# Gated SSM mix: small unfolding transfers become one VectorE transpose a unit, and two sets of coefficient transfers change queue

## The chip, the cores and the metric

The kernel runs on one core of a Trainium2 chip. The metric is device time in microseconds (us) of one execution. Three runs of the kernel before took 557.36, 558.36 and 561.56 us, median 558.36 us. The profile comes from another execution, which took 563.64 us; the traced span of it is 561.9 us.

## The reference, cut to what matters

All activations are [1, 2048, 1024] in bf16. Two sequence mixers are computed from `x` and mixed by a gate of one number per row:

```python
x = A_x
g = _sigmoid((x * gate_w).sum(-1, keepdims=True))
a = _A_ref(x, ...)   # diagonal complex state space: Bu = x B_bar; h_t = Lam_bar h_{t-1} + Bu_t
                     # y = 2 Re(h C) + x * Dskip
b = _B_ref(x, ...)   # k_shift = 4-tap causal filter of k; kv = k_shift * v
                     # y = (kv convolved with ssm_k, by FFT of length 2S) + kv * ssm_D; q * y with q = x
return g * a + (1 - g) * b
```

The change lies in the second mixer, in the long convolution of `kv` with `ssm_k`, channel by channel over 2048 time steps.

## The kernel before, in words

The kernel works on two streams of instructions at once. The **S5 stream** (branch a) does the input product, L974, L977 and L983 (with L1027 and L1030 the four-step recurrence), over 8 blocks of 128 states, spills half of the states to DRAM (`h_scr`), and later does the output product, L1180, in 16 output tiles. The **convolution stream** (branch b) treats the 1024 channels in 8 units of 128. For one unit it loads k and v transposed (L594), filters and multiplies them on VectorE and ScalarE (L767 to L782), re-sorts them by one VectorE transpose (L747), loads the unit's `ssm_k` (L596, tensor `in_B_ssm_k_dram`), and goes through two matmul stages, L792 and L814, into the spectrum. A unit's spectrum is handled in four quarters, q = 0 to 3. For a quarter a transfer pair *turns* the spectrum (two 128 KB transfers between the halves of the partitions, `turn`), VectorE multiplies the two spectra (L832), and TensorE goes back with 16 matmuls (L842, `inverse`).

Behind the inverse stands the step that changes. The result of one quarter lies in PSUM as 128 partitions by 8 by 128 values. ScalarE or VectorE copies it to a tile `qq` (L601, `evac`). Then each of the 8 slices of `qq`, 128 partitions by 128 values, is *unfolded*: one transfer of 32 KB writes it into 4 partitions of the tile `zb`, with 8 KB in each. That is 8 transfers a quarter, 32 a unit and 256 in all. When all 32 of a unit have landed, the last matmul stage of the unit can start, L871 in `final`, after the bias products L865. VectorE then multiplies by x (L877), and the result is stored to `pB_scr` or, for late units, added to the other branch (L885).

The order of the work is set by a planner that runs when the kernel is built (`_Plan.schedule`). Each operation has an engine, a planned duration, tiles that it reads and writes, and a priority from the tables at the top (`PR`); some may go to a second engine. The planner gives tiles their places in 11 slabs of SBUF of 16 KB a partition (named slab with a number in the instruction lists; one slab holds several tiles), with a cap on how many tiles of a kind live at once (`CAPS`). What comes out is a fixed order for each engine and queue. Each engine and each queue works strictly in that order. Transfers are issued from two queues, SyncE (SP) and GpSimd (POOL); in the instruction lists a queue's transfers take eight semaphores in turn (DMAHW0 to 7 on SP, DMASW0 to 7 on POOL), and a transfer waits for the one that used its semaphore before.

At the start, small vectors of coefficients are worked out on VectorE and ScalarE (L493 to L569, tiles `dco`, `cco`, `gl`). Four transfers of them (`sco<-gl`, L571) bring them to the places where L935 uses them to build diagonal matrices; four more (`sdm`, L455) load `ssm_D`. Both sets stand in the program outside the planner's list, `sco` on SP and `sdm` on ScalarE's queue.

Of the kernel before, what the change touches and what calls it, by code (L numbers as in the profile page):

```python
# [10 lines left out]
ACT = mybir.ActivationFunctionType  # L11
BF16 = mybir.dt.bfloat16
F32 = mybir.dt.float32
# [17 lines left out]
    ],  # L31
# [9 lines left out]
    ],  # L41
    "PO": [
        [-401.7, -1412.4, -159.9],
        [50.8, -104.2, 167.5],
        [-577.2, 239.1, 83.1],
        [-145.7, 329.3, -432.6],
        [-347.1, -38.2, -1031.0],
        [5.0, -1786.7, -451.4],
        [-167.3, -1738.4, -1777.2],
        [-61.5, -1003.4, -1714.9],  # L50
        [157.5, -1495.4, 707.1],
        [176.9, -2338.1, -833.4],
        [45.7, -155.1, 1169.1],
        [189.6, -2590.2, -800.3],
        [-1397.7, -1777.0, -1501.8],
        [-141.1, 180.0, 145.9],
        [-1242.8, -2235.0, -1579.5],
        [-371.1, 54.1, 18.8],
    ],
    "PC": [  # L60
        [163.7, 1215.5],
        [4.1, 1203.7],
        [292.7, 1155.8],
        [-809.1, 841.3],
        [-2711.0, 848.5],
        [-1268.2, 974.9],
        [-1197.3, 881.5],
        [-1623.9, 942.0],
    ],
# [321 lines left out]
def kernel(  # L391
# [20 lines left out]
    nc = tc.nc  # L412
# [41 lines left out]
    for i in range(4):  # L454
        nc.scalar.dma_start(out=sdm[32 * i:32 * i + 1], in_=B_ssm_D.rearrange("(o u q c) -> q o u c", o=1, q=4, c=32)[i])  # L455
# [112 lines left out]
    for k in range(2):  # L568
        cp(gco[:, :, k], cco[:, :, k:k + 2])  # L569
        for h in range(2):  # L570
            nc.sync.dma_start(out=sco[64 * k:64 * k + 64, :, h], in_=vab[64 * h:64 * h + 64, k])  # L571
# [28 lines left out]
    def evac(o_, i_, r, w, prio):  # L600
# [13 lines left out]
    CAPS = {"cA": 3, "qi": 3, "zb": 3, "Hc": 10, "tab": 26, "z": 2, "kv": 27, "qq": 13, "ra": 1, "rb": 11, "kT": 1, "vT":  # L614
            19, "acc": 7, "ka": 1, "va": 1, "pp": 1, "tmpj": 2, "t1": 2, "ot": 5, "BT": 2, "xs": 16, "dg": 3, "dp": 20,
            "tgZ": 32, "frt": 2, "rqt": 13, "Hk": 34, "CT": 9, "ga": 1}
    SPARE, NBIG, NKEEP = 9, 0, 4
# [122 lines left out]
    def conv():  # L740
# [10 lines left out]
        def load_K(u, pr, prt):  # L751
            t = pl.tile("cA", [2 * NJ, 64], cap=CAPS["cA"])
            ex = [(xT[0], 1)] if u < 2 else []
            src = B_ssm_k[u * CH:(u + 1) * CH, :].rearrange("(q c) (n m) -> q n c m", q=4, m=64)
            dma("POOL", 5.0, lambda: [t.ap[32 * q:32 * q + 32] for q in range(4)], lambda: [src[q] for q in range(4)], ex, [t], pr, n=4, alt="SP")
            op("POOL", 0.3, lambda: G.tensor_tensor(out=t.ap[:, :, 0], in0=t.ap[:, :, 0], in1=sdm[:, u, :], op=ALU.add),
               r=[t], w=[t], prio=prt)
            return t
# [76 lines left out]
        def inverse(kv, zb, q, pr):  # L835
            ps = pl.psum([8, CH])
            qq = pl.tile("qq", [8, CH], cap=CAPS["qq"])

            def f():
                for i in range(8):  # L840
# [3 lines left out]
            evac(lambda: qq.ap.rearrange("p k (c j g) -> p k c j g", c=4, g=2),  # L844
                 lambda: ps.ap.rearrange("p k (g j c) -> p k c j g", g=2, c=4), r=[ps], w=[qq], prio=pr)
            for h in range(2):
                dma("SP", 0.65, lambda h=h: [zb.ap[8 * q + 4 * h + i:128:32].rearrange("s r n c -> s (r n) c") for i in range(4)],
                    lambda h=h: [qq.ap[:, 4 * h + i] for i in range(4)], [qq], [(zb, (q, h))], pr, n=4, issue=0.6, alt="POOL", alt_issue=0.65)
# [44 lines left out]
        for u in range(NU):  # L893
# [3 lines left out]
            va = vas[u]  # L897
            zb = pl.tile("zb", [2, 16, CH], cap=CAPS["zb"])
# [4 lines left out]
            for hh in range(2):  # L903
                z = zz[hh]
                for q in (2 * hh, 2 * hh + 1):
# [6 lines left out]
                    inverse(kv, zb, q, pr + 3.0)  # L912
# [3 lines left out]
    def s5():  # L916
# [10 lines left out]
        def diag(pi, pr):  # L927
            res = []
            for tg, (a, b) in (("dp", (0, 3)), ("dg", (3, 5))):
# [13 lines left out]
                op("DVE", 0.95, mk(V), r=[e_dco], w=[dg], prio=pr, alt=("POOL", 1.9, mk(G), PUNTIL))  # L943
# [267 lines left out]
    for end in ends:  # L1211
        end()
    pl.least = {"dsk": 3, "tg1": 0, "tg2": 8, "tg3": 2, "tg4": 2, "tg5": 2, "BT": 7, "dp": 0, "dg": 5, "tab": 4, "Hc": 0,
                "grow": 4, "gb": 2, "gt": 0, "ra": 0, "rb": 0, "Hk": 0, "kT": 4, "tmpj": 0, "cA": 0, "zb": 0, "z": 0, "xs": 0,
                "Hr": 3, "CT": 2, "ot": 7, "ga": 0}
# [5 lines left out]
    order = pl.schedule({"DVE": 9.8, "ACT": 9.5, "PE": 4.6, "POOL": 3.0, "SP": 0.7})  # L1221
# [34 lines left out]
```

## Time and profile before

| | |
|---|---|
| median of 3 runs | 558.36 us (557.36 to 561.56) |
| the profiled execution, its span | 563.64 us, 561.9 us |
| TensorE (PE) matmuls | 395.5 us, 70% of the span |
| VectorE (DVE) | 287.6 us, 51% |
| ScalarE (ACT) | 251.6 us, 45% |
| GpSimd (POOL) | 189.6 us, 34% |
| the 16 DMA engines | 56.4% for SP's queue, 25.0% for POOL's |
| mean granted TensorE clock | 0.86 |

No engine is busy for the whole span, so the shares alone do not say what sets the time. The work of the two streams is spread unevenly, each engine waits in its own order, and the time is read from the gaps: which wait of TensorE is long, who releases it, and what that one waited for.

### The profile page before, as it was taken

What the parts mean: (1) busy time and instruction counts of PE and PEld (TensorE: products, weight loads), DVE (VectorE), ACT (ScalarE), POOL (GpSimd) and SP (SyncE); (2) the same over time, 40 slices, a digit from 0 to 9 for tenths busy, and PEclk for the clock granted to TensorE, in tenths of its full rate; (3) what the DMA queues carried; (4) which work ended last, traced back from release to release, by engine and by line L of the source; (5) the groups of instructions that cost most, each with busy time, mean ns of one, the idle gap of its engine ahead of it and who ended that gap; (6) DMA issues with size and microseconds to landing.
All of it is one profiled execution on the core that took longest, in us unless ns stands there. A gap on an engine that the chain in (4) does not pass through costs nothing. (4 is left out here: it accounts for less than half of the span.)

```text
span 561.9 us, 12598 instructions
## 1 busy us (share of the span) xinstructions
PE 395.5 (70%) x5195; PEld 274.3 (49%) x5216; DVE 287.6 (51%) x392; ACT 251.6 (45%) x325; POOL 189.6 (34%) x271
## 2 busy tenths in 40 slices
PE   4817989999897069497073399399937769865927
PEld 3302443444554045244062298288825658754816
DVE  2159989989993075186223280753104337613413
ACT  2009968978975036079063043275701245702000
POOL 3047500120456027014164064145611622733300
PEclk9966999999999569799576599789987888977969
DMA  6953984755879748789848999799989695997956
GB/s 123 167 93 60 147 132 86 217 151 113 152 109 111 130 122 112 82 174 223 222 57 119 145 152 104 125 187 119 124 121 128 95 145 134 107 146 88 112 112 152
DMA packets 160033, 73.01 MB, mean 130 GB/s; under 512 B 138532, under 2 KB 150852, under 8 KB 159464
## 3 DMA queue, kind: packets, MB, share of 16 engines
q1 hardware_dynamic: 147768, 49.29, 56.4%
q0 software_dynamic: 12080, 22.91, 25.0%
q8 instruction: 41, 0.67, 0.6%
q14 instruction: 16, 0.13, 0.1%
q10 hardware_dynamic: 128, 0.01, 0.0%
HBM read 19.44 MB, written 14.70 MB: 61 GB/s over the span
## 5 line engine op out<-in xcount | busy, mean ns | idle before, releaser
L601 ACT CAST slab<-ps 128x1024 bf16<-128x1024 f32 x136 | 132.1, 1031 | 176.3 <-PE ps L842 117.1
L596 POOL DMA_DIRECT2D slab<-slab x152 | 101.5, 674 | 177.8 <-ACT slab L601 106.2
L1180 PE MATMUL ps<-slab,slab 128*128 128x256 bf16 x960 | 121.5, 284 | 1.6 <-ACT slab L803 1.5
L1180 PEld LDWEIGHTS <-slab 128*128 128x128 bf16 x1024 | 103.2, 102 | 24.4 <-issue 7.6
L974 PE MATMUL ps<-slab,slab 128*128 128x512 bf16 x368 | 89.4, 391 | 25.5 <-ACT slab L601 16.1
L842 PE MATMUL ps<-slab,tG 128*128 128x128 bf16 x512 | 41.4, 252 | 61.9 <-DVE slab L832 57.7
L974 PEld LDWEIGHTS <-slab 128*128 128x128 bf16 x384 | 37.3, 100 | 73.5 <-issue 30.5
L842 PEld LDWEIGHTS <-tG 128*128 128x128 bf16 x512 | 38.4, 115 | 65.6 <-DVE slab L832 37.0
L832 DVE TENSOR_TENSOR slab<-slab 128x2048 bf16<-128x2048 bf16 x32 | 38.2, 1221 | 55.3 <-DMA slab<-slab 53.8
L803 ACT CAST slab<-ps 128x512 bf16<-128x512 f32 x96 | 49.6, 626 | 15.0 <-PE ps L792 15.0
L1189 DVE SCALAR_TENSOR_TENSOR slab<-ps,gcols,slab 128x256 bf16<-128x256 f32 x32 | 15.4, 482 | 58.0 <-PE ps L1180 36.2
L877 DVE TENSOR_TENSOR slab<-ps,slab 128x1024 bf16<-128x1024 f32 x16 | 18.9, 1220 | 41.4 <-PE ps L871 21.7
L814 PE MATMUL ps<-slab,tF 64*128 64x128 bf16 x1024 | 35.9, 228 | 4.0 <-ACT slab L803 2.0
L871 PE MATMUL ps<-slab,tabG 32*32 32x128 bf16 x1024 | 12.3, 274 | 37.3 <-DMA slab<-slab 19.4
L814 PEld LDWEIGHTS <-tF 64*128 64x128 bf16 x1024 | 32.3, 101 | 8.7 <-issue 7.2
L601 DVE CAST slab<-ps 128x1024 bf16<-128x1024 f32 x24 | 28.8, 1218 | 14.6 <-ACT slab L601 9.0
L977 PE MATMUL ps<-slab,slab 128*64 128x512 bf16 x256 | 30.4, 381 | 1.4 <-DMA slab<-in_A_B_re_dram 0.8
L803 DVE CAST slab<-ps 128x512 bf16<-128x512 f32 x32 | 20.3, 685 | 21.2 <-PE ps L792 21.2
L935 DVE TENSOR_TENSOR slab<-id,sco 128x512 bf16<-128x512 bf16 (+1 forms) x11 | 8.8, 801 | 42.2 <-DMA slab<-slab 23.8
L1185 ACT ACTIVATE slab<-ps,gcols 128x256 bf16<-128x256 f32 x31 | 14.7, 475 | 34.9 <-PE ps L1180 34.8
L871 PEld LDWEIGHTS <-tabG 32*32 32x32 bf16 x1024 | 10.4, 95 | 39.5 <-issue 23.3
L596 POOL DMA_DIRECT2D slab<-in_B_ssm_k_dram x28 | 22.1, 796 | 18.7 <-DVE slab L782 7.2
(183 smaller groups left out, 445.7 us busy)
## 6 DMA issues: line engine op xcount, KB each, us to landing
slab<-slab SPq DMA_DIRECT2D x36, 128.0 KB
slab<-slab SPq DMA_DIRECT2D x132, 32.0 KB
slab<-h_scr SPq DMA_DIRECT2D x8, 512.0 KB
slab<-slab POOLq DMA_DIRECT2D x124, 32.0 KB, 7.3
slab<-in_B_ssm_k_dram POOLq DMA_DIRECT2D x28, 128.0 KB, 6.6
slab<-slab POOLq DMA_DIRECT2D x28, 128.0 KB, 8.0
slab<-in_A_x_dram POOLq DMA_DIRECT2D x24, 128.0 KB, 8.8
h_scr<-slab POOLq DMA_DIRECT2D x3, 1024.0 KB, 5.2
```

Of the source, the lines that this page charges most:

```text
L596: QS[q].dma_start(out=o_, in_=i_)
L601: op("ACT", 1.04, lambda: A.copy(o_(), i_()), r=r, w=w, prio=prio, alt=("DVE", 1.2, lambda: V.tensor_copy(o_(), i_())))
L803: return lambda: [fn(put(hh), get(hh)) for hh in range(2)]
L814: PE_.matmul(ps.ap[:, g, i, :], lhsT=tF[64 * g:64 * g + 64, k1, 64 - 64 * r:192 - 64 * r], rhs=z.ap[64 * g:64 * g + 64, k1 % 16, r].rearra ...
L832: TT(out=t, in0=t, in1=kv.ap[:, 1].rearrange("p i c -> p (i c)").unsqueeze(1).to_broadcast([128, 2, 8 * CH]), op=ALU.mult)
L842: PE_.matmul(ps.ap[:, i], lhsT=tG[:, 8 * q + i, b, :], rhs=kv.ap[:, 2 * b, i, :], start=(b == 0), stop=(b == 1))
L871: PE_.matmul(ps[q // 2].ap[32 * e:32 * e + 32, q % 2, n], lhsT=tabG[32 * q:32 * q + 32, b, 4 * n + e, :], rhs=zb.ap[32 * q:32 * q + 32, b, ...
L877: op("DVE", 1.23, lambda h=h, hs=hs: TT(out=xs.ap[:, hs], in0=ps[h].ap.rearrange("p a g c -> p (a g) c"), in1=xs.ap[:, hs], op=ALU.mult), ...
L974: PE_.matmul(ps.ap[:, k], lhsT=BT.ap[:, d, k].rearrange("p r c -> p (r c)"), rhs=t.ap[:, d], start=(d == 0), stop=(d == ND - 1))
L977: PE_.matmul(ps.ap[64 * h:64 * h + 64, k], lhsT=BT.ap[:, d, h, k, :], rhs=t.ap[:, d], start=(d == 0), stop=False)
L1180: PE_.matmul(ps.ap, lhsT=Hr[pi].ap[:, ri, j, a * 128:(a + 1) * 128], rhs=t.ap[:, k_, ri], start=(i == 0 and ri == 0), stop=(i == NP - 1 an ...
L1189: op("DVE", 0.46, lambda: STT(out=ot.ap[:, a, :], in0=ps.ap, scalar=col(gcols, 4 * j + a), in1=ot.ap[:, a, :], op0=ALU.mult, op1=ALU.add), ...
```

## The change: what it does

The copy out of PSUM now writes a tile of the whole unit, `qq` of 64 by 32 by 2 values a partition, one quarter after the other, so that pairs of bf16 values stand side by side. When the four quarters are there, one VectorE transpose of the unit (new function `unfold`, in 32 by 32 blocks of 4-byte pairs, 2048 of them a partition) writes `zb`. The 256 unfolding transfers are gone. The transfers of `sco` and `sdm` are now operations of the planner on POOL's queue, and the operations that use them wait for them in the plan. All priorities (`PR`), the caps and the reserves of the planner have other numbers, and so the order of all the work is another; the table rows are left out here.

```diff
-    for i in range(4):
-        nc.scalar.dma_start(out=sdm[32 * i:32 * i + 1], in_=B_ssm_D.rearrange("(o u q c) -> q o u c", o=1, q=4, c=32)[i])
...
-        for h in range(2):
-            nc.sync.dma_start(out=sco[64 * k:64 * k + 64, :, h], in_=vab[64 * h:64 * h + 64, k])
...
+    kh = [(k, h) for k in range(2) for h in range(2)]
+    e_sco, e_sdm = pl.ext("sco"), pl.ext("sdm")
+    dma("POOL", 0.2, lambda: [sco[64 * k:64 * k + 64, :, h] for k, h in kh], lambda: [vab[64 * h:64 * h + 64, k] for k, h in kh], [e_dco], [e_sco],
+        -1999, n=4, alt="SP")
+    dma("POOL", 0.1, lambda: [sdm[32 * i:32 * i + 1] for i in range(4)],
+        lambda: [B_ssm_D.rearrange("(o u q c) -> q o u c", o=1, q=4, c=32)[i] for i in range(4)], [], [e_sdm], -250, n=4)
...
-        def inverse(kv, zb, q, pr):
+        def inverse(kv, qq, q, pr):
             ps = pl.psum([8, CH])
-            qq = pl.tile("qq", [8, CH], cap=CAPS["qq"])
...
-            evac(lambda: qq.ap.rearrange("p k (c j g) -> p k c j g", c=4, g=2),
-                 lambda: ps.ap.rearrange("p k (g j c) -> p k c j g", g=2, c=4), r=[ps], w=[qq], prio=pr)
-            for h in range(2):
-                dma("SP", 0.65, lambda h=h: [zb.ap[8 * q + 4 * h + i:128:32].rearrange("s r n c -> s (r n) c") for i in range(4)],
-                    lambda h=h: [qq.ap[:, 4 * h + i] for i in range(4)], [qq], [(zb, (q, h))], pr, n=4, issue=0.6, alt="POOL", alt_issue=0.65)
+            evac(lambda: qq.ap[:, :, 8 * q:8 * q + 8, :].rearrange("p (c j) k g -> p c j k g", c=4),
+                 lambda: ps.ap.rearrange("p k (g j c) -> p c j k g", g=2, c=4), r=[ps], w=[(qq, q)], prio=pr)
+
+        def unfold(qq, zb, pr):
+            def f():
+                i = qq.ap.rearrange("p c k g -> p c (k g)").bitcast(F32)
+                o = zb.ap.rearrange("p r n c -> p (r n) c").bitcast(F32).rearrange("p x c -> p c x")
+                V.transpose(o, i)
+            op("DVE", 3.75, f, r=[qq], w=[zb], prio=pr)
...
+            qq = pl.tile("qi", [64, 32, 2], cap=CAPS["qi"])
             zb = pl.tile("zb", [2, 16, CH], cap=CAPS["zb"])
...
-                    inverse(kv, zb, q, pr + 3.0)
+                    inverse(kv, qq, q, pr + 3.0)
+            unfold(qq, zb, PU[u][16])
             final(zb, u, PU[u][10:12], PU[u][12:14])
...
-                op("DVE", 0.95, mk(V), r=[e_dco], w=[dg], prio=pr, alt=("POOL", 1.9, mk(G), PUNTIL))
+                op("DVE", 0.95, mk(V), r=[e_dco, e_sco], w=[dg], prio=pr, alt=("POOL", 1.9, mk(G), PUNTIL))
```

Two places of the new order. The first is the start of the SP queue. Before, the four transfers of `sco` stand behind all loads of x but one:

```order
L594 DMA_TRANSPOSE slab_228<-in_A_x_dram 128x8x256 x2
L594 DMA_TRANSPOSE slab_229<-in_A_x_dram 128x8x256 x2
L594 DMA_TRANSPOSE slab_231<-in_A_x_dram 128x8x256
L571 DMA sco<-gl 64x8x10 x4
L594 DMA_TRANSPOSE slab_231<-in_A_x_dram 128x8x256
L594 DMA_TRANSPOSE slab_231<-in_B_k_dram 128x2048
```

Now they stand on POOL's queue (iota fills index tables, `skb` and the Dskip row are other small loads, L961 builds a table):

```order
L691 IOTA slab_218 128x32
L592 DMA skb<-in_B_shift_k_dram 128x8x4
L592 DMA sdm<-in_B_ssm_D_dram 1x8x32 x4
L592 DMA slab_218<-in_A_Dskip_dram 128x1024
L592 DMA sco<-gl 64x8x10 x4
L961 TENSOR_SCALAR slab_218<-iota_row,phn 128x512
```

SP now goes from the loads of x straight to those of k and v. The second place is the first unit's end, on VectorE. Before, a product that builds a diagonal matrix (L935) goes into a slab that holds the unit's `zb`, and waits for sixteen transfers; behind it stand the products of the spectra, L832:

```order
L601 CAST slab_234<-ps_105 128x2x4x2x64 [waits PE_49]
L1009 SCALAR_TENSOR_TENSOR slab_230<-r_160,slab_236 128x512 [waits DVE_49] x2
L935 TENSOR_TENSOR slab_232<-id_100,sco 128x768 [waits DMAHW0_49,DMAHW1_49,DMASW7_49,DMAHW2_49,DMASW6_49,DMAHW3_49,DMASW5_49,DMAHW4_49,DMASW4_49,DMAHW5_49,DMASW3_49,DMAHW6_49,DMASW2_49,DMAHW7_49,DMASW1_49,DMASW0_49]
L832 TENSOR_TENSOR slab_233<-slab_233 128x2x1024 [waits DMAHW7_49,DMAHW6_49,Activation_49]
L935 TENSOR_TENSOR slab_227<-id_100,sco 128x512
```

Now the first unit's end on VectorE reads as follows (L834 is the product of the spectra, L852 the new transpose, L882 the multiplication by x that follows the last matmuls):

```order
L834 TENSOR_TENSOR slab_224<-slab_224 128x2x1024 [waits DMASW7_49,DMASW0_49,Activation_49]
L961 TENSOR_SCALAR slab_224<-iota_row,phn 128x512
L962 TENSOR_SCALAR slab_218<-slab_224 128x512 [waits DVE_49]
L963 TENSOR_TENSOR slab_224<-slab_224,slab_218 128x512 [waits DVE_49]
L597 CAST slab_219<-ps_101 128x2x512 [waits PE_49,Activation_49]
L852 STREAM_TRANSPOSE slab_225<-slab_224 128x64x32 [waits DMASW6_49,Activation_49]
L882 TENSOR_TENSOR slab_223<-ps_104,slab_223 128x1024 [waits PE_49]
L882 TENSOR_TENSOR slab_223<-ps_101,slab_223 128x1024 [waits PE_49]
```

The transpose waits for the copies of ScalarE and one transfer, and the instruction after it on VectorE waits for TensorE alone. In the lists as a whole the transfers on SP go from 358 to 219 and those on POOL from 240 to 127; there are 64 turning transfers in both, 36 on SP and 28 on POOL before, 32 and 32 now.

## Rows read from the trace of the kernel before

**Rows 1.** The page: span; busy time, share and instructions of each engine.

```profile
span 561.9 us, 12598 instructions
PE 395.5 (70%) x5195; PEld 274.3 (49%) x5216; DVE 287.6 (51%) x392; ACT 251.6 (45%) x325; POOL 189.6 (34%) x271
```

**Rows 2.** Three windows: length; busy time per engine; granted clock, DMA share, GB/s.

```profile
46.00:180.00 134.00, 125.72 (x1077) 61.54 (x1087) 121.10 (x144) 113.72 (x126) 44.59 (x56) 0.98 0.74 132
180.00:562.00 382.00, 250.12 (x3968) 201.63 (x3976) 149.46 (x170) 130.12 (x182) 130.73 (x197) 0.82 0.87 131
532.00:541.00 9.00, 2.74 (x39) 2.14 (x36) 0.97 (x2) 0.00 (x0) 0.00 (x0) 0.88 0.33 54
```

**Rows 3.** The waits: waiting engine and line <- releaser: us, times, longest.

```profile
PE ps L842 <- DVE slab L832: 57.7, 6, 22.3
DVE slab L832 <- DMA slab<-slab: 53.8, 8, 16.3
```

**Rows 4.** Line L596 on SP: issues (ns min/median/max), then who waited (us, times).

```profile
L596 SPq DMA_DIRECT2D slab<-slab x168: 461/594/7627, 139.3 to 540.7; - x168
  PE ps L871: 36.8, 4
  DVE slab L935: 23.8, 1
```

**Rows 5.** DMA issues: transfers, KB each, median us to landing where known.

```profile
slab<-slab SPq DMA_DIRECT2D x132, 32.0 KB
slab<-slab POOLq DMA_DIRECT2D x124, 32.0 KB, 7.3
```

**Rows 6.** Timeline of the start: start us, length, engine, line [idle before <- releaser].

```profile
15.27 0.25 DVE L569 COPY gco<-cco 128x16 f32<-128x16 f32 x2
...
16.61 12.73 SPq L594 DMA_TRANSPOSE slab<-in_A_x_dram  x5
...
29.46 2.78 SPq L571 DMA_DIRECT2D sco<-gl  x4
32.28 2.08 SPq L594 DMA_TRANSPOSE slab<-in_A_x_dram  x1
33.91 0.96 DVE L935 TENSOR_TENSOR slab<-id,sco 128x768 bf16<-128x768 bf16 x1 [18.39 <-DMA sco<-gl]
...
38.88 0.23 ACT L671 ACTIVATE slab<-slab 128x32 f32<-128x32 f32 x1 [26.02 <-DVE slab L661]
```

**Rows 7.** Timeline of TensorE: five long gaps.

```profile
45.95 7.71 PE L974 MATMUL ps<-slab,slab 128*128 128x512 bf16 x24 [15.80 <-ACT slab L601]
...
202.18 3.60 PE L842 MATMUL ps<-slab,tG 128*128 128x128 bf16 x32 [22.33 <-DVE slab L832]
...
281.64 5.94 PE L842 MATMUL ps<-slab,tG 128*128 128x128 bf16 x64 [15.56 <-DVE slab L832]
...
362.62 0.61 PE L865 MATMUL ps<-slab,gl 1*128 1x128 bf16 x16 [9.04 <-DVE slab L803]
...
425.31 1.89 PE L842 MATMUL ps<-slab,tG 128*128 128x128 bf16 x16 [13.07 <-DVE slab L832]
```

**Rows 8.** Timeline of the SP queue: three stretches of issues.

```profile
291.81 21.52 SPq L596 DMA_DIRECT2D slab<-slab  x12
...
412.57 11.17 SPq L596 DMA_DIRECT2D slab<-slab  x12
...
525.98 15.29 SPq L596 DMA_DIRECT2D slab<-slab  x16
```

**Rows 9.** Groups by line and shape: busy us, mean ns of one, idle before.

```profile
L747 DVE STREAM_TRANSPOSE slab<-slab 128x1024 f32<-128x1024 f32 x8 | 16.7, 2087 | 1.2 <-PE ps L842 1.2
L596 POOL DMA_DIRECT2D slab<-slab x152 | 101.5, 674 | 177.8 <-ACT slab L601 106.2 <-DVE slab L1017 23.1 <-DMA slab<-slab 15.6
L474 ACT ACT_TABLE_LOAD x1 | 1.3, 1283 | 8.3 <-DMA sdm<-in_B_ssm_D_dram 8.3
```

**Rows 10.** Line L596 on POOL: one group of issues, ns min/median/max.

```profile
L596 POOL DMA_DIRECT2D slab<-slab x152: 518/686/1196, 142.0 to 526.3; - x152
```

More of the change, by code (lines that the diff above doesn't have):

```diff
@@ L22 @@
     "PS": [
[8 rows of a table removed]
[8 rows of a table added]
     ],
     "PU": [
[8 rows of a table removed]
[8 rows of a table added]
     ],
     "PO": [
[L43 to L58, printed above, removed]
+        [-210.2, -73.8, -86.1],
+        [-291.9, 162.6, -816.3],
+        [5.3, 3.0, 86.8],
+        [40.4, -792.0, 293.9],
+        [5.4, -665.2, -2370.0],
+        [-196.3, -138.6, -221.6],
+        [-193.1, -1372.7, 15.9],
+        [-1456.9, 411.3, -1527.6],
+        [-987.0, 96.5, -1431.0],
+        [128.3, 145.3, 120.7],
+        [235.0, 359.4, -1623.9],
+        [254.4, -728.7, -202.8],
+        [-1445.7, -121.0, -1445.7],
+        [-27.1, 250.0, 381.7],
+        [364.4, -32.7, -138.4],
+        [-1432.1, 112.6, 67.5],
     ],
     "PC": [
[L61 to L68, printed above, removed]
-    ],
-    "PH": [185.9, 238.0, 107.1, 241.4, -7.0, 244.8, 148.7, 248.2],
-    "PG": [-1217.7, -1744.7, -425.8, -200.7, 114.8, -176.6, -514.0, -1241.0],
-    "PX": [39.737, 1.001],
+        [215.4, 379.5],
+        [-242.5, 225.6],
+        [273.9, 453.1],
+        [-604.2, 20.1],
+        [23.6, 121.0],
+        [-129.4, -26.3],
+        [-876.0, 432.9],
+        [364.9, 489.1],
+    ],
+    "PH": [195.4, 194.8, 206.9, 201.9, 0.9, 209.1, -308.5, 216.3],
+    "PG": [-1045.8, -1044.5, -873.4, -710.4, -133.7, 60.4, -820.0, -1425.3],
+    "PX": [44.946, 1.039],
 }
@@ L613 @@
     PS, PU, PO, PC, PH, PG, PX = (PR[k] for k in ("PS", "PU", "PO", "PC", "PH", "PG", "PX"))
[L614 to L617, printed above, removed]
+    CAPS = {"cA": 4, "qi": 5, "zb": 17, "Hc": 4, "tab": 10, "z": 2, "kv": 4, "qq": 9, "ra": 14, "rb": 4, "kT": 2, "vT": 2,
+            "acc": 1, "ka": 1, "va": 1, "pp": 1, "tmpj": 2, "t1": 2, "ot": 3, "BT": 2, "xs": 2, "dg": 20, "dp": 14, "tgZ":
+            12, "frt": 17, "rqt": 14, "Hk": 5, "CT": 9, "ga": 7}
+    SPARE, NBIG, NKEEP = 1, 0, 4
     QB, QA = "POOL", "SP"
@@ L756, in load_K @@
             op("POOL", 0.3, lambda: G.tensor_tensor(out=t.ap[:, :, 0], in0=t.ap[:, :, 0], in1=sdm[:, u, :], op=ALU.add),
-               r=[t], w=[t], prio=prt)
+               r=[t, e_sdm], w=[t], prio=prt)
             return t
@@ L1212 @@
         end()
-    pl.least = {"dsk": 3, "tg1": 0, "tg2": 8, "tg3": 2, "tg4": 2, "tg5": 2, "BT": 7, "dp": 0, "dg": 5, "tab": 4, "Hc": 0,
-                "grow": 4, "gb": 2, "gt": 0, "ra": 0, "rb": 0, "Hk": 0, "kT": 4, "tmpj": 0, "cA": 0, "zb": 0, "z": 0, "xs": 0,
-                "Hr": 3, "CT": 2, "ot": 7, "ga": 0}
+    pl.least = {"dsk": 7, "tg1": 3, "tg2": 5, "tg5": 3, "tgZ": 3, "dp": 2, "dg": 2, "frt": 2, "rqt": 2, "tab": 0, "Hc": 2, "gb":
+                4, "gt": 0, "rb": 0, "Hk": 0, "kT": 0, "qi": 0, "zb": 0, "z": 0, "kv": 0, "xs": 5, "Hr": 0, "CT": 0, "ga": 0}
     RANK = (("ot",), ("CT", "Hr"), ("kT", "vT"), ("acc",), ("tmpj",), ("cA",), ("z",), ("kv",), ("t1",), ("qi","qq",), ("zb",), ("xs", "ga"),
@@ L1220 @@
     pl.spare, pl.nbig, pl.horizon, pl.bias = SPARE, NBIG, PX[0], PX[1]
-    order = pl.schedule({"DVE": 9.8, "ACT": 9.5, "PE": 4.6, "POOL": 3.0, "SP": 0.7})
+    order = pl.schedule({"DVE": 10.7, "ACT": 8.5, "PE": 4.6, "POOL": 3.0, "SP": 0.7})
     with tc.manual_schedule():
```

32 rows, old and new, of the table PR are left out of this document.

## The prediction

> **What bounds the kernel now.** I read the page first. TensorE is the busiest engine and still idle for 561.9 - 395.5 = 166 us; no other engine is near the span [rows 1]. So the time lies in TensorE's gaps, and the second view, the windows, says where: from 46 to 180 us TensorE works 125.7 of 134 us, beside VectorE with 121.1 and ScalarE with 113.7, while from 180 us to the end it works 250 of 382 us, and there the DMA engines are busy 0.87 of the time [rows 2]. The third view is the list of waits. TensorE's inverse (L842) waits 57.7 us, six times, for the product of spectra (L832), and that one waits 53.8 us for transfers from slab to slab, the turning transfers [rows 3]. The fourth is the SP line itself: for transfers issued there the last stage of a unit (L871) waits 36.8 us in four places, and VectorE once for 23.8 us [rows 4]. These are the transfers that the change takes away, 132 on SP and 124 on POOL [rows 5], or others that stand behind them. So the middle of the kernel is bound by computing, its start and its last two thirds by waits for transfers in order.
>
> **The change, part by part.**
>
> *The start.* The coefficients are complete at about 15.5 us, but SP issues their transfers at 29.5, behind loads of x, and VectorE gets them at 33.9; ScalarE's first table work waits behind VectorE until 38.9 [rows 6], and TensorE, its PSUM tiles full, waits 15.8 us for ScalarE's copies [rows 7]. In the new order POOL issues them and ScalarE's copies no longer stand behind that work. What is late next is the last load of x: SP ends its issue at 34.4 us now and, without the 2.8 us of `sco`, at 31.6 [rows 6]. The new start loads ScalarE's tables six times before the first copy instead of twice, four times 1.28 us, but ScalarE begins earlier, since it no longer issues `sdm`, for which it sat idle to 8.3 us [rows 9]; I take these as even, ahead of a load that is later anyway. The gain is bounded by 8 us (half the wait, if the coefficients come no sooner than about 27 us) and 16 us (the wait). I take 14, near the upper end, because the work behind the gap is short of nothing but the load of x.
>
> *The last stage of a unit.* Instead of 32 transfers, each unit has one transpose. The nearest row is the transpose L747 of 1024 pairs, 2.09 us [rows 9]; 2048 pairs cost twice that, 4.2 us. In the four places where L871 waited, 36.8 us go and at least 4 x 4.2 = 17 us of transpose stand in their place if nothing covers them: gain 20. Bounds: 36.8 if all is covered, 3 if VectorE is late by another 4.2 us each time. I take 20, by the row and without cover. The last unit shows it best: 16 issues take SP 15.3 us near the end [rows 8]; one transpose replaces them.
>
> *Products and buffers behind the transfers.* Of the 57.7 us the first gap is 22.3 us [rows 7]: VectorE stood 23.8 us [rows 4] at one instruction whose place in the slab had sixteen transfers open, all of unfolding in the order, and L832 is behind it. In the new order no instruction on VectorE, ScalarE or TensorE waits for more than five. The gap of 13.1 us at 425 [rows 7] lies behind twelve issues of 11.2 us [rows 8], eight of them unfolding. The gap of 9.0 us at 363 [rows 7] stands behind a copy that I count half. The gap of 15.6 us at 282 [rows 7] has no unfolding in front of it and stays. I take 15 of 22.3 (the turning transfers behind it may still be late), 6.5 of 13.1 and 4.5 of 9.0: 26 us. Bounds: 0, if the turning transfers were late anyway, and 44, if all three gaps go.
>
> *What it adds.* The eight transposes are 33 us of VectorE, 288 to 321 us busy. Each stands behind a unit's last inverse, and the first unit's inverses before were at 202 us [rows 7], so the transposes fall where VectorE works 149 of 382 us [rows 2]. Four are already in the second term; for the rest I add 4 us (bounds 0 and 17). The copy out of PSUM keeps its 1024 values, only the writing pattern changes, so I cost it at nothing, covered by ScalarE's idle time after 180 us. POOL loses 124 issues of 0.67 us, 84 us [rows 5, 9]; nothing on the path waits for it, so they count as nothing. POOL gets eight short transfers at the start, 8 x 0.67 = 5.4 us, and the table work behind them there is late by as much as VectorE's coefficients are; ScalarE's first copies do not need it.
>
> *The DMA engines.* In a stretch with hardly any transfers but unfolding, 9 us at a share of 0.33 and 54 GB/s [rows 2] moved 0.49 MB, 15 transfers of 32 KB: 9 x 16 x 0.33 / 15 = 3.2 us of one engine each, 256 of them 820 us, or 51 us of all sixteen. From 180 us the share falls from 0.87 to (0.87 x 382 - 51) / 340 = 0.83 even in a stretch 42 us shorter. So the engines stay loaded, and I add 11 us, about a quarter of the two gains after 46 us, for what is late next: the turning transfers behind the spills.
>
> A rule of the Trainium skill bears on this. The page DMA: Bandwidth & Descriptors (section on why a DMA increments its semaphore by 16) says that a transfer uses the largest number of engines, up to 16, that divides the slowest dimension of both sides. By that rule a transfer into 4 partitions runs on 4 engines, and unfolding loads these four with far more than their share; the trace agrees, with a share of 0.33 while almost nothing else ran. By that rule the four engines get 205 us back rather than 51, the 11 us fall away, and the sum would be 11 us lower.
>
> Sum: 563.6 - 14 - 20 - 26 + 4 + 11 = 518.6 us against the profiled execution. That one is 5.3 us above the median of the runs, so the forecast for the median is 513 us.
>
> **The rivals.**
>
> *A, the transfers stay the bound.* The turning transfers were late because of spills and transposing loads, not of unfolding. For it: the gap at 282 us, with no unfolding in front, and the DMA share of 0.87 [rows 2, 7]. Against it: SP's stretches of 21.5 and 11.2 us of issues [rows 8]. Then only the start and half the second term come: 563.6 - 14 - 10 + 4 - 5.3 = 538 us.
>
> *B, all of it goes.* The engines that unfolding filled set every transfer's landing, so the three gaps go whole, the transposes are covered, and nothing new is late: 563.6 - 16 - 36.8 - 44 - 5.3 = 461 us at the far end; half the way from the forecast to it, 487 us, is what I give it. For it: L871's and L935's waits [rows 4]. The Trainium skill's rule on engines, above, speaks for this one.
>
> *C, slower: VectorE becomes the wait.* Strictly in order, each transpose stands at the head of VectorE until the last copy of its unit is done, and the products and scans behind it wait. If a head wait is as long as L871's mean wait now, 36.8 / 4 = 9.2 us [rows 4], plus 4.2 us of transpose, eight cost 107 us against gains of 60: 563.6 - 60 + 107 - 5.3 = 605 us. It decides from 60 / 8 = 7.5 us a unit. Against it: in the new order the instruction ahead of the first transpose is VectorE's own copy, and after 180 us VectorE is idle 60% of the time [rows 2].
>
> *D, POOL is starved.* The turning transfers on POOL are held up by VectorE's transposes, up to 8 x 4.2 = 33 us: 513 + 33 = 546 us. Against it: of 152 issues on POOL none took more than 1.20 us, against a median of 0.69 [rows 10], beside a VectorE that was busy half the time. The Trainium skill says this on the page SBUF - State Buffer (section SBUF: two separate sides): a GpSimd-issued transfer cannot get its descriptors written while VectorE holds the shared port in a fast mode. The trace does not show that here.
>
> *E, no difference.* The gains at the start and the end are taken back by a worse order in between: all priorities changed, and the middle is bound by computing whatever the transfers do. That needs about 45 us of new waits; nothing in the profile names a place for it. 558 us. That the change does not do what it says is excluded: no unfolding transfer is left in the order.
>
> **How the numbers follow.** Forecast 0.55, A 0.17, B 0.14, C 0.05, D 0.03, E 0.06. The predicted time is 513 us. If every term went half way to its bound in one direction, the forecast would be 487 or 544 us; since they will not all err one way, its own range is 495 to 531. 8 in 10 reaches to B below and A above: 485 to 543 us. One per cent, 5.6 us, is about what can be told from no change. Faster by more: the forecast, A, B, D and a little less for doubt, 0.87. The same 0.07, slower 0.06.
>
> **What would show it.** In the new trace: `sco` issued by POOL at 20 us or so, TensorE's gap near 30 us at most 3 us; eight transposes of about 4.2 us; no wait of the last stage for a transfer, and under 6 us for the transpose; VectorE's 23.8 us wait gone; SP's time on transfers between slabs down by three quarters; DMA share near 0.75. It is wrong if L834 still waits 50 us for turning transfers (A), or if TensorE's waits name VectorE's transpose (C).

## The result, and the profile after

The changed kernel takes 433.7 us (median of 4 runs, 428.9 to 438.2) against 560.0 us before on the same chip: a ratio of 0.767, 95% interval 0.761 to 0.773. The forecast was 513 us with a range from 485 to 543, so the direction was right and the gain came out at 126 us where I had 45. The profiled execution of the changed kernel is one of its slower ones (438.2 us); medians, here and below, are of all runs of a kernel, ratios and intervals leave out runs more than 1.5% above its fastest.

The page of the changed kernel: span; busy time, share and instructions of each engine.

```profile
span 436.4 us, 12122 instructions
PE 379.6 (87%) x5216; PEld 260.4 (60%) x5216; DVE 311.6 (71%) x395; ACT 254.0 (58%) x333; POOL 112.3 (26%) x159
```

Against [rows 1] the span is 125.5 us shorter. TensorE's idle time falls from 166.4 to 56.8 us, which gives 109.6; its busy time falls by 15.9, which I had not counted at all.

Two windows of the changed kernel, columns as in [rows 2]:

```profile
46.00:180.00 134.00, 117.05 (x1033) 57.70 (x1032) 116.43 (x135) 85.95 (x102) 34.34 (x43) 0.94 0.75 135
180.00:436.00 256.00, 228.13 (x3929) 184.74 (x3924) 164.81 (x166) 137.99 (x196) 48.44 (x81) 0.97 0.83 154
```

From 180 us on TensorE now works 0.89 of the time instead of 0.65, at a granted clock of 0.97 instead of 0.82. The DMA share there is 0.83, the number that the prediction gave for a longer stretch, and still the waits for transfers are nearly gone, as the groups below show: that the engines are loaded on the mean was not what bound the kernel.

Where the idle time went shows in TensorE's groups. First those of the kernel before (line, names, shapes, count | busy us, mean ns of one | idle before it, by releaser):

```profile
L974 PE MATMUL ps<-slab,slab 128*128 128x512 bf16 x368 | 89.4, 391 | 25.5 <-ACT slab L601 16.1 <-DVE t_a L539 5.6 <-DMA slab<-in_A_x_dram 2.5
...
L842 PE MATMUL ps<-slab,tG 128*128 128x128 bf16 x512 | 41.4, 252 | 61.9 <-DVE slab L832 57.7 <-issue 4.0 <-ACT slab L601 0.2
...
L1180 PE MATMUL ps<-slab 128*128 128x256 bf16 x64 | 13.5, 292 | 6.0 <-DMA slab<-in_A_C_im_dram 6.0
...
L871 PE MATMUL ps<-slab,tabG 32*32 32x128 bf16 x1024 | 12.3, 274 | 37.3 <-DMA slab<-slab 19.4 <-DMA out_dram<-slab 10.3 <-DMA slab<-in_B_ssm_k_dram 7.1
...
L865 PE MATMUL ps<-slab,gl 1*128 1x128 bf16 x128 | 4.3, 259 | 10.0 <-DVE slab L803 9.8
```

The same groups of the changed kernel, where L981 stands for L974, L843 for L842, L876 for L871, L870 for L865 and L1187 for L1180 (128 matmuls of this form instead of 64):

```profile
L981 PE MATMUL ps<-slab,slab 128*128 128x512 bf16 x368 | 85.2, 386 | 8.1 <-DVE dco L550 5.1 <-DMA slab<-in_A_x_dram 3.0
...
L843 PE MATMUL ps<-slab,tG 128*128 128x128 bf16 x512 | 34.6, 226 | 12.9 <-DVE slab L834 11.5 <-ACT slab L805 0.8 <-ACT slab L597 0.6
...
L1187 PE MATMUL ps<-slab 128*128 128x256 bf16 x128 | 23.2, 273 | 1.1 <-ACT slab L805 1.1
...
L876 PE MATMUL ps<-slab,tabG 32*32 32x128 bf16 x1024 | 11.0, 229 | 2.4 <-issue 2.4
...
L870 PE MATMUL ps<-slab,gl 1*128 1x128 bf16 x128 | 3.7, 227 | 1.1 <-ACT slab L805 1.1
```

Idle time falls by 17.4 us at the start (L981), 49.0 at the inverse, 34.9 at the last stage and 8.9 at its first half (L870), and by 4.9 at the output stage. Single matmuls are shorter too, 226 instead of 252 ns in the inverse, at the higher clock.

VectorE's groups of the product (L834, L832 before) and of the new transpose, columns as above:

```profile
L834 DVE TENSOR_TENSOR slab<-slab 128x2048 bf16<-128x2048 bf16 x32 | 38.2, 1214 | 2.7 <-DMA slab<-slab 2.7
...
L852 DVE STREAM_TRANSPOSE slab<-slab 128x2048 f32<-128x2048 f32 x8 | 29.9, 3734 | 12.4 <-PE ps L816 7.1 <-ACT slab L597 5.1
```

The issues between slabs, all of them turning transfers now (ns min/median/max):

```profile
L592 POOL DMA_DIRECT2D slab<-slab x32: 516/526/557, 128.6 to 372.4; - x32
L592 SPq DMA_DIRECT2D slab<-slab x32: 461/550/3050, 131.3 to 398.8; - x32
```

The turning transfers on POOL in the list of DMA issues (KB each, median us from issue to landing), first before, then now:

```profile
slab<-slab POOLq DMA_DIRECT2D x28, 128.0 KB, 8.0
```

```profile
slab<-slab POOLq DMA_DIRECT2D x32, 128.0 KB, 4.3
```

The timeline of the start, columns as in [rows 6]:

```profile
17.77 3.31 POOL L592 DMA_DIRECT2D sco<-gl  x4 [10.09 <-DVE gco L567]
...
27.27 10.53 PE L981 MATMUL ps<-slab,slab 128*128 128x512 bf16 x48 [3.01 <-DMA slab<-in_A_x_dram]
```

The product waits 2.7 us for turning transfers where it waited 53.8 [rows 3]. The transposes wait 12.4 us themselves, but no one waits long for them. The longest issue on SP of this kind is 3.1 us instead of 7.6 [rows 4]. At the start all is as forecast: coefficients issued by POOL at 17.8 us, then a gap of 3.0 us behind a load of x where 15.8 us stood [rows 7].

### The profile page after: what moved, and what is told of

It reads as the page before. It is cut to its first block, busy times and chain, and to the rows that moved or that the text cites. A ratio compares the mean times of both kernels' runs of the same rounds, so it can differ in the third digit from the quotient of the medians.

```text
span 436.4 us, 12122 instructions
## 1 busy us (share of the span) xinstructions
PE 379.6 (87%) x5216; PEld 260.4 (60%) x5216; DVE 311.6 (71%) x395; ACT 254.0 (58%) x333; POOL 112.3 (26%) x159
## 4 chain that ended last, share of the span: by engine, by line
PE 63%; ACT 12%; DVE 11%; DMA 9%; issue 4%; POOL 1%; SPq 0%; DVEq 0%; ACTq 0%; POOLq 0%
PE ps L1187 24%; PE ps L981 14%; DMA slab<-in_B_k_dram 6%; PE ps L984 5%; PE ps L843 5%; ACT slab L597 5%; PE ps L816 5%; PE ps L1034 3%; ACT slab L805 3%; PE ps L876 2%; PE ps L990 2%; DMA sco<-gl 2%; DMA slab<-slab 1%; PE ps L794 1%; DVE slab L834 1%
## 5 line engine op out<-in xcount | busy, mean ns | idle before, releaser
L1187 PE MATMUL ps<-slab,slab 128*128 128x256 bf16 x896 | 108.4, 273 | 0.6 <-ACT slab L805 0.5
L1187 PEld LDWEIGHTS <-slab 128*128 128x128 bf16 x1024 | 98.2, 98 | 14.9 <-issue 1.9
L981 PE MATMUL ps<-slab,slab 128*128 128x512 bf16 x368 | 85.2, 386 | 8.1 <-DVE dco L550 5.1
L981 PEld LDWEIGHTS <-slab 128*128 128x128 bf16 x384 | 37.0, 99 | 55.8 <-DMA slab<-in_A_x_dram 8.9
L843 PE MATMUL ps<-slab,tG 128*128 128x128 bf16 x512 | 34.6, 226 | 12.9 <-DVE slab L834 11.5
L597 DVE CAST slab<-ps 128x1024 bf16<-128x1024 f32 x19 | 23.2, 1221 | 29.0 <-PE ps L816 14.6
L843 PEld LDWEIGHTS <-tG 128*128 128x128 bf16 x512 | 31.9, 102 | 16.0 <-DVE slab L834 12.0
L834 DVE TENSOR_TENSOR slab<-slab 128x2048 bf16<-128x2048 bf16 x32 | 38.2, 1214 | 2.7 <-DMA slab<-slab 2.7
L852 DVE STREAM_TRANSPOSE slab<-slab 128x2048 f32<-128x2048 f32 x8 | 29.9, 3734 | 12.4 <-PE ps L816 7.1
L592 POOL DMA_DIRECT2D slab<-slab x32 | 16.8, 530 | 78.8 <-ACT slab L597 78.0
L794 PE MATMUL ps<-tab,slab 64*128 64x128 bf16 x512 | 21.7, 219 | 11.7 <-DVE slab L749 3.2
L794 PEld LDWEIGHTS <-slab 64*128 64x128 bf16 x512 | 15.8, 95 | 20.2 <-issue 14.9
L1034 PE MATMUL ps<-slab,slab 128*128 128x512 bf16 x96 | 25.2, 390 | 1.1 <-ACT slab L597 1.1
L984 PEld LDWEIGHTS <-slab 128*64 128x64 bf16 x256 | 16.0, 120 | 16.6 <-issue 7.3
```

The lines of the kernel that those rows point to most:

```text
L592: QS[q].dma_start(out=o_, in_=i_)
L597: op("ACT", 1.04, lambda: A.copy(o_(), i_()), r=r, w=w, prio=prio, alt=("DVE", 1.2, lambda: V.tensor_copy(o_(), i_())))
L794: PE_.matmul(ps.ap[:, t, i, :], lhsT=a.ap[64 * t:64 * t + 64, c:c + 2].rearrange("p g n -> p (g n)"), rhs=t1v[64 * t:64 * t + 64], start=T ...
L834: TT(out=t, in0=t, in1=kv.ap[:, 1].rearrange("p i c -> p (i c)").unsqueeze(1).to_broadcast([128, 2, 8 * CH]), op=ALU.mult)
L843: PE_.matmul(ps.ap[:, i], lhsT=tG[:, 8 * q + i, b, :], rhs=kv.ap[:, 2 * b, i, :], start=(b == 0), stop=(b == 1))
L852: V.transpose(o, i)
```

## Experiments

Medians are of 4 or more runs, beside the kernel before on the same chip each time (559 to 561 us); single runs scatter by about 1%, so differences of 5 us between two kernels are not told apart. Two questions: do the transfers carry the surplus over the forecast, or the new order with all its priorities? And if the transfers, by what?

### The transfers, or the order

**b_trans**: the order of before, transfers out, transposes in.

```diff
-            for h in range(2):
-                dma("SP", 0.65, lambda h=h: [zb.ap[8 * q + 4 * h + i:128:32].rearrange("s r n c -> s (r n) c") for i in range(4)],
...
+            def un(h, qn):
+                zb.left -= 1
+                if zb.left == 0:
+                    for t in zb.qs:
+                        V.tensor_copy(zb.ap[:, 0, 0, 0:2], t.ap[:, 0, 0:2])
+                    V.transpose(zb.ap.rearrange("p r n c -> p (r n) c").bitcast(F32).rearrange("p x c -> p c x"),
+                                tG[:, 0:16].rearrange("p a b c -> p (a b c)").bitcast(F32).rearrange("p (c k) -> p c k", k=32))
```

> The kernel before in its own order, instruction for instruction, without the 256 unfolding transfers: at the place of each unit's last one VectorE does one transpose of 2048 pairs (the size of the changed kernel's) and four tiny copies that make it wait for the unit's four copies out of PSUM. The transpose reads a constant table, so the unfolded values are left out. Theory T (the transfers themselves held up everything that stood in a queue with them or waited for a buffer; the new order is worth little): 430 to 465 us, SP's and VectorE's waits for transfers mostly gone. Theory O (the transfers cost the 45 us of the forecast, and the rest of the gain is the new order's): 505 to 540 us.

Measured 445.5 us, ratio 0.796 (0.789 to 0.804). Theory T.

**a_burst**: the order of the changed kernel, transfers back in place of each transpose.

```diff
-                V.transpose(o, i)
+                for k in range(32):
+                    QS["SP" if k // 4 % 2 else "POOL"].dma_start(out=zb.ap[k:128:32].rearrange("s r n c -> s (r n) c"), in_=w[:, k])
```

> The changed kernel in its own order, but the copies out of PSUM write the layout of before and at the place of each transpose stand the 32 unfolding transfers of before, 16 on SP and 16 on POOL. Theory T: 530 us or more, TensorE waiting again for turning transfers and for the unfolded unit. Theory O: 450 to 480 us, a few us of wait behind each burst and no more.

Measured 568.9 us, ratio 1.014 (1.002 to 1.026). The group of the last stage in its trace, columns as above:

```profile
L876 PE MATMUL ps<-slab,tabG 32*32 32x128 bf16 x1024 | 12.1, 283 | 122.5 <-DMA slab<-slab 66.2
```

The new order with the old transfers is no faster than the old kernel. Theory T again.

**after_transfers**: the inverse and the transfers of before under the changed kernel's tables, with the order planned anew.

```diff
-                    inverse(kv, qq, q, pr + 3.0)
-            unfold(qq, zb, PU[u][16])
+                    inverse(kv, zb, q, pr + 3.0)
```

> The changed kernel's tables and limits, with the unfolding transfers of before put back quarter by quarter and the order planned anew with them. Theory T: 530 to 580 us, near the kernel before. Theory O: 450 to 490 us, since the tables carry the gain.

Measured 560.8 us, ratio 1.006 (1.001 to 1.011). Theory O does not hold: the new tables are worth nothing while the transfers stand. They even cost something, as the next kernel shows.

**b_coef**: the coefficients alone.

```diff
-        nc.scalar.dma_start(out=sdm[32 * i:32 * i + 1], in_=B_ssm_D.rearrange("(o u q c) -> q o u c", o=1, q=4, c=32)[i])
+        nc.gpsimd.dma_start(out=sdm[32 * i:32 * i + 1], in_=B_ssm_D.rearrange("(o u q c) -> q o u c", o=1, q=4, c=32)[i])
...
-            nc.sync.dma_start(out=sco[64 * k:64 * k + 64, :, h], in_=vab[64 * h:64 * h + 64, k])
+            nc.gpsimd.dma_start(out=sco[64 * k:64 * k + 64, :, h], in_=vab[64 * h:64 * h + 64, k])
```

> The kernel before with the coefficient transfers (four of sco, four of sdm) issued by GpSimd at the places where SP and ScalarE issued them; nothing else. The forecast's term for the start was 14 us (8 to 16). If it holds alone: 542 to 552 us. If the start's gain needs the new order or is taken back later by the transfers: 555 to 563 us.

Measured 541.9 us, ratio 0.970 (0.961 to 0.980), a gain of 18 us (11 to 22): the forecast's term of 14, kept to the end of the program. The kernel after_transfers has the coefficients on POOL's queue too, and early, as its trace shows:

```profile
17.76 3.31 POOL L592 DMA_DIRECT2D sco<-gl  x4 [10.04 <-DVE gco L567]
```

Yet it takes 560.8 us where b_coef takes 541.9. So with the transfers in place the new tables lose about 19 us, all that the coefficients gain.

**b_trans_coef**: the edits of b_trans and b_coef together, in the order of before.

> b_trans with b_coef's edit as well: before's order, transposes of a constant table in place of the transfers (the unfolded values are left out), coefficients issued by GpSimd. If the two effects are all of the change and add up: 0.796 x 0.970 x 560 = 433 us, the time of the changed kernel, whose order is another. If they overlap: 440 to 447 us. If the new order hides a loss or a gain of its own, this differs from the changed kernel's 430 by more than 10 us.

Measured 430.6 us, ratio 0.770 (0.763 to 0.777). That is the changed kernel's time in the old order. The two edits make up the whole gain, and they add up (0.796 x 0.970 = 0.772); without the transfers the new order neither gains nor loses anything that can be measured.

**b_none** and **a_none**: no unfolding at all, in the order of before and of the change.

```diff
-                                           rhs=zb.ap[32 * q:32 * q + 32, b, 4 * n + e, :], start=False, stop=(n == 3 and b == 1),
+                                           rhs=tG[32 * q:32 * q + 32, 4 * n + e, b, :], start=False, stop=(n == 3 and b == 1),
...
-                V.transpose(o, i)
```

> b_trans without its eight transposes and their tiny copies, the last stage reading a constant table (nothing is unfolded). The forecast counted 17 + 4 = 21 us for the transposes, 30 us of VectorE's time in all. If they are on the path as forecast: 424 us. If all are covered, as L881's wait of 0.0 us in b_trans says: 440 to 447 us.

> The changed kernel without its eight transposes, the last stage reading a constant table (nothing is unfolded). If the 21 us of the forecast for transposes are on the path: 409 us. If all are covered, as the wait of the last stage of 2.4 us in the changed kernel's trace says: 425 to 431 us.

Measured 438.8 us, ratio 0.782 (0.772 to 0.791), and 431.5 us, ratio 0.768 (0.760 to 0.775). Eight transposes cost about 7 us in the old order, with intervals that overlap a little, and nothing that can be measured in the new one.

### What in the transfers

The next kernels put 256 transfers back into b_trans, or take one thing from the kernel before.

**b_trans_d16c**, **b_trans_d4c**, **b_trans_d4q**: transfers that nobody waits for, into DRAM.

```diff
+    u_scr = [dram.tile([4, 33, 128], BF16, name=f"u_scr{i}") for i in range(256)]
...
+                for i in range(4):
+                    un_n.append(0)
+                    QS[qn].dma_start(out=u_scr[len(un_n) - 1][:, 0:32, :], in_=qq.ap[:, 4 * h + i])
```

This is b_trans_d4q. In b_trans_d4c the source is `tF[:, len(un_n) % 32, 0:128]`, and in b_trans_d16c the target also is `u_scr[len(un_n) - 1].rearrange("a b c -> (a b) c")[0:128]`.

> As b_trans_d4c, the same 256 issues of 32 KB with the same 128 pieces of 256 bytes each, but the DRAM side has 128 rows instead of 4. Theory E4 (a shape of 4 rows keeps each transfer on few engines, which then hold up everything): 445 to 475 us. Theory S (the number of issues in order, each waiting for the eighth before it, costs the time, whatever the shape): within 10 us of b_trans_d4c.

> As b_trans_d4q, but the 256 transfers read a constant table: they wait for no copy and hold no buffer; only queue places and engines are taken. Theory E: within 15 us of b_trans_d4q, 505 to 560 us. Theory B (the wait of a transfer at the head of SP and POOL for its copy out of PSUM, and the buffers it holds, cost the time): 445 to 470 us. Theory W: 445 to 460 us.

> b_trans, and at their places in the queues the 256 transfers again, same source, bytes and 4-row shape, but into a DRAM buffer of 4 rows that nobody reads: a transfer still waits for its copy and holds its source buffer and its place in the queue, but the last stage waits for none. Theory E (the transfers load few engines or land late, and whatever is behind them in the queues is late with them): 520 to 560 us. Theory W (the time went in those who waited for unfolded data): 445 to 470 us.

Measured 459.5 us (ratio 0.821, 0.814 to 0.829), 486.6 us (0.871, 0.864 to 0.878) and 489.6 us (0.874, 0.866 to 0.883). So 256 issues and their bytes cost 14 us, four rows instead of 128 another 27, and the waits for copies out of PSUM nothing that shows. No theory named the whole: b_trans_d4q falls between the ranges of E and W, B and S are refuted, and E4 is right about the step from b_trans_d4c to b_trans_d16c, but 70 us to the kernel before remained.

**b_trans_s16q** and **b_trans_s4q**: the same into a part of SBUF that nothing reads.

```diff
-                    QS[qn].dma_start(out=u_scr[len(un_n) - 1][:, 0:32, :], in_=qq.ap[:, 4 * h + i])
+                    QS[qn].dma_start(out=slabs[NSLAB - 1][8 * q + 4 * h + i:128:32, 2048:5120].rearrange("s (r c) -> s r c", r=32), in_=qq.ap[:, 4 * h + i, 0:96])
```

This is b_trans_s4q; in b_trans_s16q the target is a piece of 96 columns of the same place over all 128 rows.

> As b_trans_d4q, but the 256 transfers go into 4 rows of a part of SBUF that nothing reads or reuses (96 of each 128 elements, so 192-byte pieces, as many pieces as before). Theory D (a transfer into SBUF of 4 rows is slower than one into DRAM, and part of the 70 us is that): 505 to 540 us. Theory R (the target is no matter; the rest is in waits for the unfolded tile and its place): 480 to 495 us.

> As b_trans_s4q (same source, 256 issues, 128 pieces of 192 bytes each, into a part of SBUF that nothing reads), but the target has 128 rows instead of 4. Theory E4 (4 rows are what makes the transfers hold up everything): 455 to 470 us, like b_trans_d16c. Theory D (any transfer from SBUF into SBUF of this number is slow): within 15 us of b_trans_s4q, 503 to 530 us.

Measured 517.4 us (ratio 0.924, 0.916 to 0.931) and 468.1 us (468.1 / 561.2 = 0.834; this one came without an interval). Same source, pieces and bytes: the four rows alone cost 49 us, as theory E4 has it and theory D, for b_trans_s16q, has not. The traces show what they change. The issues on POOL (ns min/median/max), first of b_trans_s16q, then of b_trans_s4q:

```profile
L853 POOL DMA_DIRECT2D slab<-slab x124: 534/534/1019, 151.3 to 434.3; - x124
```

```profile
L853 POOL DMA_DIRECT2D slab<-slab x124: 683/683/1197, 151.9 to 489.8; - x124
```

Issue to landing on POOL (KB each, median us) of the turning transfers and of these, again b_trans_s16q first:

```profile
slab<-slab POOLq DMA_DIRECT2D x28, 128.0 KB, 4.5
...
slab<-slab POOLq DMA_DIRECT2D x124, 24.0 KB, 3.4
```

```profile
slab<-slab POOLq DMA_DIRECT2D x28, 128.0 KB, 7.3
...
slab<-slab POOLq DMA_DIRECT2D x124, 24.0 KB, 6.1
```

The waits of the product (L833 in both) and of the inverse (L843), columns as in [rows 3], in the same sequence:

```profile
DVE slab L833 <- DMA slab<-slab: 11.3, 4, 5.8
...
PE ps L843 <- DVE slab L833: 8.6, 7, 3.2
```

```profile
DVE slab L833 <- DMA slab<-slab: 58.4, 12, 19.3
PE ps L843 <- DVE slab L833: 51.2, 8, 18.6
```

With four rows the transfers land after 6.1 us instead of 3.4, and the turning transfers, which are the same in both, after 7.3 instead of 4.5, near the 8.0 us of the kernel before. The inverse waits 51.2 us, nearly the 57.7 of [rows 3], in a kernel where no one waits for unfolded data. Issue and landing both grew, and these two kernels do not tell how much of the 49 us is due to which.

**b_final_const** and **b_final_const96**: the kernel before, its transfers whole or at 96 of 128 elements, the last stage reading a table (edit as in b_none).

> The kernel before with all its transfers, but the last stage of a unit (L871) reads a constant table in place of the unfolded tile (the unfolded values are left out), so TensorE waits for no unfolding transfer; whoever writes over an unfolded tile's place still waits for its transfers. Between b_trans_d4q (490) and before (560) lie 70 us. Theory W (TensorE's own waits at L871 are what is left, 36.8 us in the trace): 515 to 530 us. Theory P (the waits for places in the slabs, and transfers that land late behind one another, are the rest; L871's waits only show them): 545 to 560 us. Theory W+ (all 70 us are L871's): 490 to 500 us.

> b_final_const (nobody on TensorE waits for unfolding; the unfolded values are left out) with transfers of 96 of each 128 elements, the sizes of b_trans_s4q. It differs from b_trans_s4q in the waits for the places of unfolded tiles, and in the transposes (7 us). Theory R (waits for the places make the 32 us between the two): 540 to 550 us. Theory Y (the bytes make it, 24 KB against 32 KB a transfer): 505 to 515 us.

Measured 549.7 us (ratio 0.973, 0.964 to 0.983) and 533.7 us (0.951, 0.943 to 0.960). Taking away every wait of TensorE for an unfolded tile gains 10 us by the medians, 15 (10 to 20) by the ratio, not the 36.8 that stood at L871. The wait goes elsewhere, as the inverse of b_final_const shows:

```profile
L842 PE MATMUL ps<-slab,tG 128*128 128x128 bf16 x512 | 40.2, 248 | 80.7 <-DVE slab L832 76.8 <-issue 3.6 <-ACT slab L601 0.2
```

It idles 80.7 us where 61.9 stood: the turning transfers are late either way. So theory P held for b_final_const. For the last 32 us neither R nor Y alone: without the 7 us of transposes b_trans_s4q stands at 511, so 23 us (533.7 - 510.7) are left for the waits for places, and the bytes make 16 (549.7 - 533.7). That the 23 us are such waits is a remainder and not shown: the two kernels also write to other places, and the 7 us were measured elsewhere.

The ladder from no unfolding to the kernel before: 438.8, plus 23 for 256 transfers of 128 rows (468.1 - 445.5), plus 49 for their four rows, plus 23 left for places in the slabs, plus 16 for 32 KB instead of 24, plus 10 for the last stage's own wait, gives 560. It has to, since each step is the difference of two neighbours; by the ratios the last two are 12 and 15, so a step is good to some 5 us. The steps were measured in this sequence; in another they may share differently.

## Why the prediction was wrong

*What bounds the kernel* was read rightly: TensorE's gaps, and transfers in order behind most of them.

*The start* was right: 14 us forecast (8 to 16), 18 measured alone, 17.4 in TensorE's idle time, with the load of x late next as said.

*Products and buffers behind the transfers* is the step that failed, with *The DMA engines* that priced it from the other side. I followed each gap back one step and asked whether an unfolding transfer stood directly in front. So I took only 26 us off the waits for the product and for one copy, half of the copy's wait, and of the gap of 15.6 us at 282 I wrote that it "has no unfolding in front of it and stays". Then 11 us were added "for what is late next". The runs show 49.0 us gone at the inverse, 8.9 at the first half of the last stage, 4.9 at the output, and nothing late next that took them back.

The gap at 282 shows the mistake. SP's queue in the kernel before (start us, length, line, count; slab<-h_scr are the reloads of spilled states), and VectorE's product:

```profile
205.85 22.99 SPq L596 DMA_DIRECT2D slab<-slab  x20
...
246.22 5.83 SPq L596 DMA_DIRECT2D slab<-h_scr  x8
254.73 1.16 SPq L596 DMA_DIRECT2D slab<-slab  x2
```

```profile
278.09 4.63 DVE L832 TENSOR_TENSOR slab<-slab 128x2048 bf16<-128x2048 bf16 x4 [16.33 <-DMA slab<-slab]
```

The same place in b_trans:

```profile
211.03 7.75 SPq L596 DMA_DIRECT2D slab<-h_scr  x8
226.47 1.15 SPq L596 DMA_DIRECT2D slab<-slab  x2
```

```profile
237.79 4.63 DVE L832 TENSOR_TENSOR slab<-slab 128x2048 bf16<-128x2048 bf16 x4 [4.29 <-issue]
...
241.34 6.08 PE L842 MATMUL ps<-slab,tG 128*128 128x128 bf16 x64 [3.52 <-DVE slab L832]
```

In the kernel before SP spends 23 us on 20 unfolding issues (b_trans has none in that stretch), and reaches the 8 reloads of 512 KB only 8.5 us before the turning transfers; their product starts 23.4 us after the turning's issue. In b_trans the reloads start 15.4 us ahead, the product comes after 11.3, and TensorE's gap is 3.5 us instead of 15.6. The gap stood behind other transfers than unfolding, near to what rival A said. But these came 35 us later than in b_trans, 23 of them spent on unfolding issues that begin 40 us further up the same queue.

*The DMA engines*: I counted what the engines get back as a mean, 51 us of sixteen, and took from it that they stay loaded. The share after 180 us did come out at 0.83, but by luck: that was for a stretch of 340 us, and with the 256 us that it became, the same sum gives (0.87 x 382 - 51) / 256 = 1.10. (The sign "DMA share near 0.75" did not come either.) The DMA queues of b_trans, SP's first: packets, MB, share of sixteen engines:

```profile
q1 hardware_dynamic: 130344, 44.96, 53.5%
q0 software_dynamic: 6128, 18.64, 18.7%
```

These are 72.2% of 444.9 us, 321 us of all sixteen; before it was 81.4% of 561.9, 457. So the transfers, with what they slowed down in others, took 136 us, or 8.5 us of one engine each, where 3.2 had been read from a stretch with hardly any other traffic. Besides, what counted was not the mean but the landing of a transfer that others stand behind: 4.3 us for the turning transfers on POOL, 8.0 before.

The Trainium skill's page DMA: Bandwidth & Descriptors (section on why a DMA increments its semaphore by 16) says that the slowest dimension of the two sides, here the four rows, limits how many engines a transfer uses. The runs agree in direction: 4 rows against 128, at the same bytes and pieces, 517 against 468 us and 6.1 against 3.4 us to land. I cited that rule and let it move 11 us; it deserved the larger part of the chance. That all 256 transfers shared the same four engines, as the 205 us had it, no run shows. No row names the engines of a transfer, but SP's queue hints at their number, first in b_trans_s16q, then in b_trans_s4q:

```profile
q1 hardware_dynamic: 149352, 48.21, 55.3%
```

```profile
q1 hardware_dynamic: 147768, 48.21, 56.5%
```

Four rows take 1584 packets fewer, 12 for each of SP's 132 transfers. Sixteen engines against four, with one closing packet each, would do that; it is not shown that this is the reason.

*The last stage of a unit*: 20 forecast, 34.9 us of idle time gone (37.3 to 2.4). But that wait alone, with the transfers left, is worth 10 to 20 us; for the most part it was one more place where the same lateness came to light, not a cost of its own.

*What it adds*: 21 us of transposes, 17 of them inside the term above, were 0 to 7. "Without cover" was the wrong choice: the idle time of TensorE before L876 is 2.4 us, and none of it names the transpose. One transpose was also sized too long, 4.2 us against 3.73 measured.

*Not in the sum*: TensorE's busy time, 15.9 us. It goes with the transfers: b_trans, in the order of before, has 382.7 us where 395.5 stood. Four windows of the kernel before, in and behind the gap at 282, columns as in [rows 2]:

```profile
270.00:278.00 8.00, 0.00 (x0) 0.00 (x0) 0.00 (x0) 0.00 (x0) 0.54 (x1) 0.50 1.03 268
278.00:282.00 4.00, 0.36 (x4) 0.36 (x4) 3.91 (x4) 0.00 (x0) 0.00 (x0) 0.50 0.20 81
282.00:286.00 4.00, 4.00 (x41) 4.00 (x39) 0.72 (x1) 1.77 (x2) 0.32 (x1) 0.50 0.00 0
286.00:290.00 4.00, 2.64 (x57) 2.37 (x55) 0.04 (x1) 2.74 (x5) 3.98 (x7) 0.96 0.44 65
```

TensorE stands idle for 8 us at a granted clock of 0.50, the level of 1.2 GHz, and works the 4 us from 282 at that level with no pause before 0.96 is granted: 41 matmuls there, 57 in the 2.64 busy us that follow. A gap costs its own length and some slow work behind it. But the short gap can cost as much slow work as the long one; here is the same inverse in b_trans, behind its gap of 3.5 us:

```profile
242.00:246.00 4.00, 4.00 (x41) 4.00 (x39) 0.42 (x1) 2.02 (x2) 2.36 (x5) 0.50 0.72 217
```

So which gaps gave back the 15.9 us is not shown.

Of the rivals, B was the right one and its far end, 461 us, was still 27 us too long: the gap at 282 and the busy time were missing from it, 15.6 + 15.9 us. Its mechanism, that unfolding sets when every other transfer lands, is what the runs show. C, VectorE as the wait, and D, POOL starved by it, did not come: the turning issues on POOL lasted 516 to 557 ns in the changed kernel. E, a worse order that takes the gains back, is what after_transfers shows, 560.8 us against the 541.9 of b_coef; with the transfers gone, as in the change, it does not come: 430.6 us in the old order, 433.7 in the new one.

## What to carry to other kernels

When transfers in order bound a kernel, do not price one kind of transfer by who waits for it last. Ask what its issues push back in the queue and in landing time, also 40 us earlier; a consumer's wait can be taken away whole (36.8 us here) and give back only 10 to 20 us. Many transfers into a few rows are the first to replace by an engine's own instruction, even one that adds 30 us of busy time to that engine, if it has idle time where the data is due.

## What the runs showed of the hardware

- Rows of the target matter at equal bytes and pieces: 24 KB into 4 rows of SBUF took POOL 683 ns to issue and 6.1 us to land, into 128 rows 534 ns and 3.4 us.
- Four rows in SBUF cost more than four in DRAM: 517 us with 24 KB a transfer, in pieces of 192 bytes, against 490 with 32 KB in pieces of 256.
- One transpose of 2048 pairs of bf16 took 3.73 us, less than twice the 2.09 us of 1024 pairs [rows 9].
